# Zero-weight filler matmuls in TensorE's idle stretches of a two-block attention kernel

## The chip, the cores and the metric

The kernel runs on one core of one Trainium2 chip. The metric is device time in microseconds (us) from the first to the last instruction of the core, lower is better. A profiled span can differ from the median by some us, so each number below says which it is.

## The reference

Two blocks run twice each over a sequence of 2048 with 512 features. Block A is softmax attention with 32 query heads of 16 and one shared key/value head; block B is linear attention.

```python
def _A_ref(x, wq, wk, wv, wo):                 # H = 32, Dh = 16
    q = (x @ wq).reshape(B, S, H, Dh).transpose(0, 2, 1, 3)
    k, v = x @ wk, x @ wv
    p = softmax(einsum("bhqd,bkd->bhqk", q, k) * Dh ** -0.5)
    o = einsum("bhqk,bkd->bhqd", p, v)
    return o.transpose(0, 2, 1, 3).reshape(B, S, H * Dh) @ wo
def _B_ref(x, wqkv, wo):
    ...                                        # phi(q) (phi(k)^T v) / (phi(q) sum phi(k)), then @ wo
x = x + _A_ref(layernorm(x), ...)
x = x + _B_ref(layernorm(x), ...)
x = x + _A_ref(layernorm(x), ...)
x = x + _B_ref(layernorm(x), ...)
```

## The kernel before

A small scheduler in the kernel file plans the whole program before it is emitted. It keeps a model time, gives each operation a modelled duration, and starts on each free engine the ready operation of the best priority. The result is a fixed order for each engine, with semaphore waits between them. On the chip each engine runs its list in order. When TensorE (PE) is free in the model and events are left, it calls a hook:

```python
class Sched:
    def run(self):
        while True:
            ...                                # start what is ready
            if self.tfree[PE] <= self.now + 1e-9 and self.events:
                self.idle(self.now)
    ...
    def emit(self, name, eng):
        for o in self.order[name]:
            ...                                # waits
            ins = o.fn(eng)
            ...                                # semaphore increment
```

The attention work flows like this. PE makes up to three score tiles of 128x512 in PSUM banks 0-2 or 3-5. ScalarE (ACT) takes the exponential of all three at once into `PTA`. PE then multiplies them with V (the PV matmuls) into the accumulator bank 7. Some tiles go by bank 6 to VectorE (DVE), which makes the exponential into `PTD` with one operation for each tile (0.69 us in the page below) and six for a pair of tiles (0.42 to 1.21 us each). After 64 PV matmuls the bank is complete, and it is copied out to `Eo`. Until that copy is done no PV matmul of the next unit may start.

```python
# scores of m tiles, then one exponential
o  = add(PE, 0.05 + 0.14 * m, f, ..., prio=0.0, name="sA")
oe = add(AC, tac(m * 512), lambda e: e.activation(PTA[...], bank(3 * s, m * 512), ACTF.Exp, scale=SCALE), ...)
# PV, into 32 of the 128 partitions of bank 7
return e.matmul(ps[32 * c:32 * c + 32, 7 * 512:8 * 512], lhsT=Vaug[:, kt, :], rhs=src,
                start=opened[0], stop=opened[1], skip_group_check=True)
# the copy that frees bank 7
oe = add((DV, AC), ..., ev, deps=[last], acq=[he], uses=[h7], rel=[h7], prio=0.0, name="evA")

DUMMY = 0.0
def idle(now):
    if ctl.layer is None or ctl.ramp or ctl.tail or DUMMY <= 0:
        credit[0], credit[1] = 0.0, now
        return                                 # with DUMMY = 0 nothing is ever added
    ...
sc.idle = idle
```

The softmax here doesn't subtract the row's maximum and nothing guards it: scores larger than these inputs give would overflow.

## Time and profile before

| | before |
|---|---|
| time, three runs | 1869.71 us median (1867.76 to 1870.54) |
| profiled span, mean granted PE clock | 1878.3 us, 0.966 |
| start to first exponential | 15.4 us |
| first attention (start of the first to start of the last ACT exponential) | 888.7 us |
| layer tail and next start | 39.9 us |
| second attention | 888.3 us |
| last tail | 46.0 us |

These are lines of the profile page of the kernel before: busy time by engine, the granted clock in 40 slices, and two groups (line, engine, operation, names, shapes, count, then busy us, mean ns, and the idle time before them with what ended it).

```profile
PE 1656.9 (88%) x10339; PEld 487.6 (26%) x10408; DVE 1670.1 (89%) x2991; ACT 1738.2 (93%) x1525; POOL 33.7 (2%) x46
...
PEclk9999999996999989999899999999999998999998
...
L775 ACT ACTIVATE PTA<-ps_all 128x1536 bf16<-128x1536 f32 (+1 forms) x1265 | 1638.7, 1403 | 84.8 <-PE ps_all L635 79.2
L635 PE MATMUL ps_all<-QT,Kr 64*128 64x512 bf16 x4096 | 864.9, 392 | 135.5 <-ACT PTA L775 85.0
```

ACT is the fullest engine. PE's 88% should not be read as full: in this trace matmuls recorded as 392 ns long (the mean of L635) start some 215 to 227 ns apart at full clock, where they do not start together, so the records overlap. At half clock they start 390 to 426 ns apart. From these starts I estimate what PE's array does: I take a matmul as its columns at 2.4 for each ns (512 columns in the shortest steady spacing of 215 ns are 2.38) times the granted clock, and merge overlaps. By this estimate the array streams for about 1225 us of the 1878; with the median spacing of 222 ns it would be 1267. It counts the 256 float32 transposes of 128 columns short: in this trace they start 108 to 169 ns apart at full clock, not 53.

The clock records of the kernel before hold two levels only, 1.00 and 0.50. Its 17 stretches at 0.50 are 127 us together, and each, but for the last, which the trace's end cuts, is a whole number of 3.413 us long: one such length (3.41 us) to four (13.65 us), and one of ten (34.13 us). The stretches at full clock between them are whole numbers of it too. I call such a length a window, and the part of it that is covered by the estimate above its streaming share. The deepest dip of the clock line (the 6 in its tenth slice, about 423 to 470 us) is the stretch of ten windows; in it the array was covered to 0.72 to 0.89 of each window, and the clock stayed at 0.50 all the same. The next table looks there.

Here is the windows table of the kernel before (stretch and length, then busy us and count of PE, PEld, DVE, ACT, POOL, then granted clock, DMA share, GB/s). The first two stretches are slow ones, the third is calm.

```profile
430.00:440.00 10.00, 10.00 (x35) 1.57 (x32) 4.24 (x9) 5.80 (x4) 0.00 (x0) 0.50 0.00 0
440.00:450.00 10.00, 10.00 (x39) 1.84 (x38) 7.39 (x12) 7.82 (x6) 0.00 (x0) 0.50 0.00 0
580.00:590.00 10.00, 9.61 (x63) 2.80 (x61) 9.97 (x19) 10.00 (x9) 0.00 (x0) 1.00 0.00 0
```

At a clock of 0.50 PE looks fully busy, and ACT and DVE starve. The timeline of the kernel before shows why (start us, length us, engine, line, and count of the merged matmuls), first at half clock, then at full clock:

```profile
455.05 1.03 PE L635 MATMUL ps_all<-QT,Kr 64*128 64x512 bf16 x3
456.01 0.61 PE L671 MATMUL ps_all<-PTA,Vaug 128*32 128x512 bf16 x3
456.55 1.03 PE L635 MATMUL ps_all<-QT,Kr 64*128 64x512 bf16 x3
...
901.77 0.61 PE L635 MATMUL ps_all<-QT,Kr 64*128 64x512 bf16 x3 [0.42 <-ACT PTA L775]
902.31 0.40 PE L671 MATMUL ps_all<-PTA,Vaug 128*32 128x512 bf16 x3
```

At half clock one round of three scores and three PV takes 456.55 - 455.05 = 1.50 us, a little more than the 1.48 us exponential that it feeds (the mean of its form of 1536 columns), with nothing left for other work. At full clock PE has pauses, as the one of 0.42 us above.

And this is what came before a drop, in the timeline of the kernel before (the clock fell at 657.8):

```profile
655.38 0.60 PE L635 MATMUL ps_all<-QT,Kr 64*128 64x512 bf16 x4 [0.42 <-ACT PTA L775]
656.51 0.68 DVE L683 COPY Eo<-ps_all 128x512 f32<-128x512 f32 x1
657.25 0.09 PEld L671 LDWEIGHTS ps_all<-PTD,Vaug 128*32 128x32 bf16 x1 [1.75 <-DVE Eo L683]
657.25 0.39 PE L671 MATMUL ps_all<-PTD,Vaug 128*32 128x512 bf16 x1 [1.26 <-DVE Eo L683]
```

The accumulator is full, its copy to `Eo` starts late, and PE stands for 1.26 us. In the window before each of the twelve drops inside attention the longest pause of the array was 1.0 to 1.4 us for ten drops and 0.7 and 0.6 us for the other two, at a streaming share of 0.32 to 0.49.

### The profile page before, as it was taken

What the parts mean: (1) busy time and instruction counts of PE and PEld (TensorE: products, weight loads), DVE (VectorE), ACT (ScalarE), POOL (GpSimd) and SP (SyncE); (2) the same over time, 40 slices, a digit from 0 to 9 for tenths busy, and PEclk for the clock granted to TensorE, in tenths of its full rate; (3) what the DMA queues carried; (4) which work ended last, traced back from release to release, by engine and by line L of the source; (5) the groups of instructions that cost most, each with busy time, mean ns of one, the idle gap of its engine ahead of it and who ended that gap; (6) DMA issues with size and microseconds to landing.
All of it is one profiled execution on the core that took longest, in us unless ns stands there. A gap on an engine that the chain in (4) does not pass through costs nothing.

```text
span 1878.3 us, 25542 instructions
## 1 busy us (share of the span) xinstructions
PE 1656.9 (88%) x10339; PEld 487.6 (26%) x10408; DVE 1670.1 (89%) x2991; ACT 1738.2 (93%) x1525; POOL 33.7 (2%) x46
## 2 busy tenths in 40 slices
PE   7889899889998899899688899988989888998887
PEld 4222222221222223222342222222222222222223
DVE  7999989997889988998689999899998899989975
ACT  7999999997899989999689999999999999999995
POOL 0000000000000000000000000000000000000000
PEclk9999999996999989999899999999999998999998
DMA  3000000000000000000000000000000000000001
GB/s 113 1 1 1 1 1 1 1 1 1 1 1 1 1 1 1 1 1 1 0 1 1 1 1 1 1 1 1 1 1 1 1 1 1 1 1 1 1 1 45
DMA packets 7717, 9.00 MB, mean 5 GB/s; under 512 B 1456, under 2 KB 7088, under 8 KB 7600
## 3 DMA queue, kind: packets, MB, share of 16 engines
q1 hardware_dynamic: 7600, 7.37, 1.2%
q8 instruction: 81, 1.33, 0.3%
q14 instruction: 36, 0.29, 0.0%
HBM read 5.28 MB, written 2.10 MB: 4 GB/s over the span
## 4 chain that ended last, share of the span: by engine, by line
DVE 48%; PE 38%; ACT 10%; issue 2%; DMA 0%; POOL 0%; SPq 0%
PE ps_all L635 15%; PE ps_all L671 12%; DVE xT L829 11%; DVE PTD L851 9%; ACT PTA L775 9%; PE ps_all L496 7%; DVE xs L847 5%; DVE xs L850 5%; DVE xu L846 5%; DVE xu L849 3%; DVE xs L848 2%; PE ps_all L692 1%; DVE Eo L683 1%; DVE stats L461 1%; PE ps_all L1049 1%
## 5 line engine op out<-in xcount | busy, mean ns | idle before, releaser
L775 ACT ACTIVATE PTA<-ps_all 128x1536 bf16<-128x1536 f32 (+1 forms) x1265 | 1638.7, 1403 | 84.8 <-PE ps_all L635 79.2
L635 PE MATMUL ps_all<-QT,Kr 64*128 64x512 bf16 x4096 | 864.9, 392 | 135.5 <-ACT PTA L775 85.0
L671 PE MATMUL ps_all<-PTA,Vaug 128*32 128x512 bf16 x3567 | 559.5, 396 | 6.9 <-DVE Eo L683 5.0
L829 DVE TENSOR_SCALAR xT<-ps_all 128x512 int32<-128x512 f32 x529 | 362.3, 685 | 64.2 <-PE ps_all L635 62.0
L635 PEld LDWEIGHTS ps_all<-QT,Kr 64*128 64x128 bf16 x4096 | 179.5, 94 | 606.4 <-ACT PTA L775 283.9
L851 DVE SCALAR_TENSOR_TENSOR PTD<-xT,xs 128x1024 uint16<-128x1024 int32 x265 | 321.8, 1214 | 1.4
L671 PEld LDWEIGHTS ps_all<-PTA,Vaug 128*32 128x32 bf16 x3567 | 133.0, 93 | 485.7 <-issue 467.4
L846 DVE TENSOR_SCALAR xu<-xT 128x1024 f16<-128x1024 uint16 x265 | 181.8, 686 | 2.9
L850 DVE TENSOR_TENSOR xs<-xs,xu 128x1024 f16<-128x1024 f16 x265 | 180.8, 682 | 2.5
L847 DVE TENSOR_TENSOR xs<-xu 128x1024 f16<-128x1024 f16 x265 | 180.2, 680 | 1.4
L671 PE MATMUL ps_all<-PTD,Vaug 128*32 128x512 bf16 x529 | 148.5, 403 | 22.7 <-DVE Eo L683 16.9
L848 DVE TENSOR_SCALAR xs<-xs 128x1024 f16<-128x1024 f16 x265 | 110.3, 416 | 1.7
L849 DVE TENSOR_SCALAR xu<-xu 128x1024 f16<-128x1024 f16 x265 | 110.5, 417 | 0.0
L496 PE MATMUL ps_all<-wqkv_sb,xnT 128*128 128x512 bf16 x231 | 67.9, 398 | 6.1 <-issue 2.3
L469 POOL TENSOR_TENSOR rstd<-veps,mhalf 128x1 f32<-128x1 f32 x30 | 30.1, 1006 | 1764.6 <-DVE veps L467 1759.7
L671 PEld LDWEIGHTS ps_all<-PTD,Vaug 128*32 128x32 bf16 x529 | 32.1, 95 | 84.1 <-DVE Eo L683 28.9
L692 PE MATMUL ps_all<-identf,Eo 128*128 128x128 f32 x256 | 46.8, 311 | 6.2 <-DVE Eo L683 4.7
L928 ACT ACTIVATE e_buf<-ps_all 128x512 f32<-128x512 f32 x64 | 39.1, 610 | 12.9 <-PE ps_all L496 9.1
L683 DVE COPY Eo<-ps_all 128x512 f32<-128x512 f32 x62 | 42.4, 684 | 8.6 <-PE ps_all L671 8.5
L461 DVE BATCH_NORM_STATS2 stats<-x_sb 128x6 f32<-128x512 bf16 x64 | 42.9, 679 | 3.4 <-DMA x_sb<-in_A_x_dram 3.2
L929 DVE TENSOR_SCALAR e_buf<-e_buf 128x512 f32<-128x512 f32 x64 | 26.9, 420 | 20.7 <-ACT e_buf L928 20.6
L947 DVE CAST v_tok<-ps_all 128x512 bf16<-128x512 f32 x32 | 22.0, 688 | 25.0 <-PE ps_all L496 24.7
(85 smaller groups left out, 783.2 us busy)
## 6 DMA issues: line engine op xcount, KB each, us to landing
out_dram<-x_sb SPq DMA_DIRECT2D x16, 128.0 KB, 1.7
x_sb<-in_A_x_dram SPq DMA_DIRECT2D x3, 512.0 KB, 7.4
wqkv_sb<-in_B_wqkv_dram SPq DMA_DIRECT2D x1, 1536.0 KB, 11.8
x_sb<-in_A_x_dram SPq DMA_DIRECT2D x2, 256.0 KB, 3.1
wq_sb<-in_A_wq_dram SPq DMA_DIRECT2D x1, 512.0 KB, 5.1
wo_sb<-in_A_wo_dram SPq DMA_DIRECT2D x1, 512.0 KB, 9.2
wo_sb<-in_B_wo_dram SPq DMA_DIRECT2D x1, 512.0 KB, 10.9
wk_sb<-in_A_wk_dram SPq DMA_DIRECT2D x1, 16.0 KB, 2.5
```

The lines of the kernel that those rows point to most:

```text
L496: i = e.matmul(bank(h.idx, n), lhsT=l, rhs=r, start=(c + k == 0), stop=(c + k == len(mms) - 1))
L635: x = e.matmul(bank(b0 + k), lhsT=Kr[r, m, kt * P:(kt + 1) * P], rhs=QT[r, self.units[u][0] % 2, gs, q0:q0 + n], start=True, stop=True)
L671: return e.matmul(ps[32 * c:32 * c + 32, 7 * 512:8 * 512], lhsT=Vaug[:, kt, :], rhs=src, start=opened[0], stop=opened[1], skip_group_check ...
L692: i = e.transpose(bank(ht.idx, P, qs * P), Eo[:, he.idx, qs * P:(qs + 1) * P], identf[:])
L775: oe = add(AC, tac(m * 512), lambda e: e.activation(PTA[:, hp.idx, 0:m * 512], bank(3 * s, m * 512), ACTF.Exp, scale=SCALE), deps=[o] + pr ...
L829: o = add(DV, tdv(512), lambda e: e.tensor_scalar(out=xT[:, hx.idx, i * 512:(i + 1) * 512], in0=bank(6), scalar1=SCALE * LOG2E * 65536.0, ...
L846: o = add(DV, tdv(w, 0.52), lambda e: e.tensor_scalar(out=u_, in0=lo, scalar1=1.0 / 65536, scalar2=-0.5, op0=ALU.mult, op1=ALU.add), deps= ...
L847: o1 = add(DV, tdv(w, 0.52), lambda e: e.tensor_tensor(out=s_, in0=u_, in1=u_, op=ALU.mult), deps=[o] + c["prev"], name="xsq", **kw)
L848: o2 = add(DV, tdv(w, 0.26), lambda e: e.tensor_scalar(out=s_, in0=s_, scalar1=XK, scalar2=-XW, op0=ALU.mult, op1=ALU.add), deps=[o1], nam ...
L849: o3 = add(DV, tdv(w, 0.26), lambda e: e.tensor_scalar(out=u_, in0=u_, scalar1=1.0, scalar2=XL, op0=ALU.mult, op1=ALU.add), deps=[o1], nam ...
L850: o4 = add(DV, tdv(w, 0.52), lambda e: e.tensor_tensor(out=s_, in0=s_, in1=u_, op=ALU.mult), deps=[o2, o3], name="xc", **kw)
L851: o5 = add(DV, tdv(w), lambda e: e.scalar_tensor_tensor(out=PTD[:, hp.idx, 0:w].bitcast(U16), in0=xT[:, k, 0:w], scalar=2.0 ** -9, in1=s_, ...
```

## The change

The hook now adds filler matmuls: 512 columns of a finite constant tile, with 128x128 zero weights, into bank 7. The intent is to fill pauses like those before the drops. If the bank holds a running sum, the filler adds zero to it; if the bank is free, it starts a group there, and the first PV of the next unit overwrites it. A filler is planned where the model has PE idle and finds under 0.6 of the last 1.7 us streaming. It is not planned while the bank waits for its copy.

```diff
-    DUMMY = 0.0
+    FILL, FILLW, FILLN = 0.6, 1.7, 512
-    zer = sb("zer", [P, 240], BF16)
+    zer = sb("zer", [P, P], BF16)
+    def streaming(now):
+        tot = 0.0
+        for o in reversed(sc.order[PE]):
+            if o.t0 + 1.5 < now - FILLW:
+                break
+            st = {"pv": 0.071, "sA": 0.4, "dummy": 0.2}.get(o.name, 0.85 * o.dur[PE])
+            ...
+        return tot
     def idle(now):
-        if ctl.layer is None or ctl.ramp or ctl.tail or DUMMY <= 0:
-        ...
+        if not sc.order[PE] or streaming(now) > FILL * FILLW:
             return
         u = ctl.acc_owner
-        if credit[0] < 0.1 or u < 0 or not 0 < sum(ctl.count[u]) < 64:
+        owned = u >= 0 and 0 < sum(ctl.count[u]) < 64
+        if not owned and not banks.free[7]:
             return
+        if owned and now < sc.tfree[AC] < now + 0.1:
+            return
-        o = add(PE, 0.11, ... e.matmul(bank(7, 240, 272), lhsT=ident[:], rhs=zer[:], start=False, ...
+        o = add(PE, 0.03 + FILLN * 0.41e-3, lambda e: e.matmul(bank(7, FILLN), lhsT=zer[:],
+                rhs=maskx[:].bitcast(BF16)[:, 0:FILLN], start=not owned, stop=True, ...),
+                ..., prio=9.0, name="dummy")
```

Two things change: fillers run on PE, and their modelled 0.24 us shift the plan, so the order of the real work on PE, ACT and DVE is another one.

More of the change, by code (lines that the diff above doesn't have):

```diff
@@ L874, in bass_interleave_layers__grouped_kv_mqa__linear_attn_block__prompt_kernel @@
     sc.step = ctl.step
-    credit = [0.0, 0.0]
+    def streaming(now):
[4 more added lines that the diff above has]
+            st = {"pv": 0.071, "sA": 0.4, "dummy": 0.2}.get(o.name, 0.85 * o.dur[PE])
+            end = o.t0 + o.dur[PE]
+            if end > now - FILLW:
+                tot += st * min(1.0, (end - (now - FILLW)) / o.dur[PE])
+        return tot
     def idle(now):
-        if ctl.layer is None or ctl.ramp or ctl.tail or DUMMY <= 0:
-            credit[0], credit[1] = 0.0, now
+        if not sc.order[PE] or streaming(now) > FILL * FILLW:
             return
-        credit[0] = min(2.0, credit[0] + (now - credit[1]) * DUMMY)
-        credit[1] = now
         u = ctl.acc_owner
-        if credit[0] < 0.1 or u < 0 or not 0 < sum(ctl.count[u]) < 64:
+        owned = u >= 0 and 0 < sum(ctl.count[u]) < 64
+        if not owned and not banks.free[7]:
             return
-        credit[0] -= 0.1
-        o = add(PE, 0.11, lambda e: e.matmul(bank(7, 240, 272), lhsT=ident[:], rhs=zer[:], start=False, stop=True, skip_group_check=True),
-                reads=["ident", "zer"], prio=9.0, name="dummy")
+        if owned and now < sc.tfree[AC] < now + 0.1:
+            return
+        o = add(PE, 0.03 + FILLN * 0.41e-3, lambda e: e.matmul(bank(7, FILLN), lhsT=zer[:], rhs=maskx[:].bitcast(BF16)[:, 0:FILLN], start=not owned, stop=True, skip_group_check=True),
+                reads=["mask", "zer"], deps=[] if owned else list(banks.hist[7]), prio=9.0, name="dummy")
+        banks.hist[7].append(o)
         sc._try(PE)
```

## The prediction

> **What bounds the kernel now.** In the two attention stages (about 40–900 and 930–1826 us) ACT and DVE share the softmax exponentials and both are nearly full: the windows table gives ACT 97–98% and DVE 95–98% in calm stretches such as 560:650 and 1230:1300. TensorE (88% busy on the page) is not full: [...]I find its array idle for about 640 us of 1878. So TensorE matters only where it makes the others wait.
>
> It does so where its clock falls. The mean granted clock is 0.966; the clock records show about 17 stretches at exactly 0.50, together 127 us, nearly all 3.4 or 6.8 us long, one of 34 us (426:460). [...]the window before a drop was not empty: its streaming share was 0.32–0.49, where the mean of all windows is 0.65. At half clock three scores take 1.03 us on the timeline and not 0.60, three PV matmuls 0.61 and not 0.40, and one round of both takes 1.5 us, more than the 1.48 us exponential that it feeds.
>
> **What the drops cost.** In the twelve drops inside attention (plus 2.5 us of margin each) ACT idles 34 us and DVE 31 us where the calm rate would give 4–6; so about 27 us. The two layer tails (907:917, 1835:1856) run their serial chain at half clock: 4 transposes 0.61 us, projection matmuls 0.43 us each; about 3 us each, 6 us. Ceiling: some 33 us, 1.8%.
>
> **What the change adds.** Matmuls 128x512 of zero weights into bank 7, wherever the schedule's own model sees under 0.6 of the last 1.7 us streaming and TensorE idle. No work leaves. I estimate 500–1000 of them (attention alone models at about 0.5–0.55, the whole at 0.65), 0.215 us of array each, 110–215 us, against 640 us idle. [...] Estimated cost 3–12 us.
>
> **What it does not reach.** Most drops begin at a bank-7 turnover: TensorE waits 1.0–1.4 us for the DVE eviction (Eo, line 683; e.g. before 375, 426, 555, 658, 1313, 1562). Then bank 7 is neither owned nor free, so no filler may go there; only the rest of the 3.4 us window can be raised. I expect half-clock time to fall from 127 us to 20–60 us, not to nothing, and the long 34 us one to go. Gain 20–28 us, less cost 3–12.
>
> **Prediction.** 1852 us, 80% range 1830 to 1872. Faster by over 2%: 0.10; within 2%: 0.86; slower by over 2%: 0.04.
>
> **What would show it.** Right: mean clock 0.985 or more; half-clock time under 60 us; the exponential's idle before it (80 us on scores) falls by 15–25 us; ACT busy time unchanged. The filler group has 500–1000 instructions. Wrong: clock near 1 but time unchanged (then fillers delay scores: the exponential's waits for scores grow outside the former drops); or clock unchanged (then fillers sit at the wrong places[...]).
>
> **What would make it wrong.** The schedule model runs faster than the chip (its exponential is 1.37 us, the trace's 1.48), so fillers may land where the chip has no gap; the greedy schedule may shift as a whole by some us; more fillers than estimated; or a clock drop costing more than its own ACT idle.

Passages that no trace of this case shows are cut and marked, here and in the expectation of E4. No term of the sum is cut: the middles of 20 to 28 us gained and 3 to 12 us lost are 24 and 7.5, together some 16 us, from 1869 us to the forecast of 1852. The 640 us idle are read in the way told above (1878 less 1225 are 653).

## The result, and the profile after

The kernel after takes 1850.72 us median (1847.09 to 1853.99, four runs), the one before 1868.93 us beside it. The ratio is 0.9902 with a 95% interval of 0.9881 to 0.9922. By the 2% rule that is "same", and it is clear of noise.

| | before | after |
|---|---|---|
| profiled span, clock | 1878.3 us, 0.966 | 1845.4 us, 1.000 |
| start to first exponential | 15.4 | 14.5 |
| first attention | 888.7 | 874.0 |
| tail and next start | 39.9 | 35.7 |
| second attention | 888.3 | 879.6 |
| last tail | 46.0 | 41.6 |

The page of the kernel after, the same lines and the new group:

```profile
PE 1754.5 (95%) x11002; PEld 515.1 (28%) x11002; DVE 1658.7 (90%) x2966; ACT 1739.9 (94%) x1529; POOL 34.2 (2%) x46
...
PEclk9999999999999999999999999999999999999999
...
L775 ACT ACTIVATE PTA<-ps_all 128x1536 bf16<-128x1536 f32 (+1 forms) x1268 | 1640.6, 1398 | 59.4 <-PE ps_all L635 52.1
L635 PE MATMUL ps_all<-QT,Kr 64*128 64x512 bf16 x4096 | 835.1, 383 | 42.0 <-DVE xT L829 16.0
...
L897 PE MATMUL ps_all<-maskx,zer 128*128 128x512 bf16 x594 | 205.0, 387 | 0.0
```

ACT does the same work (1739.9 us, 1738.2 before) with less idle time before its exponentials (59.4 us, 84.8 before). The clock line has no dip. PE is busier by fillers, and its span is shorter all the same.

The windows table of the kernel after, at the stretches shown of before:

```profile
430.00:440.00 10.00, 10.00 (x60) 2.54 (x57) 9.41 (x16) 9.37 (x8) 0.00 (x0) 1.00 0.00 0
440.00:450.00 10.00, 9.11 (x55) 2.35 (x53) 9.97 (x17) 9.98 (x9) 0.00 (x0) 1.00 0.01 2
580.00:590.00 10.00, 9.88 (x56) 2.47 (x55) 9.90 (x17) 10.00 (x8) 0.00 (x0) 1.00 0.00 0
```

I also cut both traces into windows of 3.413 us (before, in step with the ends of its clock's stretches), and counted the windows at full clock, from the first exponential on, by their streaming share. Before, 23 had a share under 0.45 and 10 of those were followed by a drop; 45 had a share under 0.50, and 16 of those were followed by one. After, 4 and 8 are left, and none was followed by a drop. The lowest share rose from 0.19 to 0.41. (With the float32 transposes counted twice, the counts are 17 and 41 before, 1 and 5 after, with the same drops. With 222 ns for 512 columns they are 18 and 33 before, 10 and 14 of them followed by a drop, and 2 and 6 after, none of them. The reading does not hang on it, but the shares do by some hundredths.)

A copy of bank 7 still stops PE. In the timeline of the kernel after, around one of them:

```profile
372.03 0.60 PE L635 MATMUL ps_all<-QT,Kr 64*128 64x512 bf16 x3 [0.35 <-ACT PTA L775]
372.11 0.69 DVE L683 COPY Eo<-ps_all 128x512 f32<-128x512 f32 x1
372.85 0.42 PEld L692 LDWEIGHTS ps_all<-identf,Eo 128*128 128x128 f32 x4 [0.71 <-DVE Eo L683]
```

No filler stands there, as the rule demands: of the 594, none started during any of the 64 copies.

### The profile page after: what moved, and what is told of

Its sections match the earlier page's. It is cut to its first block, busy times and chain, and to the rows that moved or that the text cites. A ratio compares the mean times of both kernels' runs of the same rounds, so it can differ in the third digit from the quotient of the medians.

```text
span 1845.4 us, 26741 instructions
## 1 busy us (share of the span) xinstructions
PE 1754.5 (95%) x11002; PEld 515.1 (28%) x11002; DVE 1658.7 (90%) x2966; ACT 1739.9 (94%) x1529; POOL 34.2 (2%) x46
## 4 chain that ended last, share of the span: by engine, by line
PE 44%; DVE 43%; ACT 11%; issue 1%; POOL 1%; DMA 0%; SPq 0%
PE ps_all L635 17%; PE ps_all L671 13%; ACT PTA L775 10%; DVE xT L829 9%; DVE PTD L851 8%; PE ps_all L496 7%; DVE xs L850 5%; DVE xs L847 5%; DVE xu L846 4%; DVE xu L849 3%; DVE xs L848 2%; PE ps_all L897 2%; PE ps_all L692 1%; DVE Eo L683 1%; DVE stats L461 1%
## 5 line engine op out<-in xcount | busy, mean ns | idle before, releaser
L775 ACT ACTIVATE PTA<-ps_all 128x1536 bf16<-128x1536 f32 (+1 forms) x1268 | 1640.6, 1398 | 59.4 <-PE ps_all L635 52.1
L635 PE MATMUL ps_all<-QT,Kr 64*128 64x512 bf16 x4096 | 835.1, 383 | 42.0 <-DVE xT L829 16.0
L671 PE MATMUL ps_all<-PTA,Vaug 128*32 128x512 bf16 x3573 | 539.3, 389 | 3.4 <-DVE Eo L683 2.8
L851 DVE SCALAR_TENSOR_TENSOR PTD<-xT,xs 128x1024 uint16<-128x1024 int32 (+1 forms) x262 | 318.4, 1215 | 1.4
L897 PE MATMUL ps_all<-maskx,zer 128*128 128x512 bf16 x594 | 205.0, 387 | 0.0
L846 DVE TENSOR_SCALAR xu<-xT 128x1024 f16<-128x1024 uint16 (+1 forms) x262 | 180.2, 688 | 3.0
L850 DVE TENSOR_TENSOR xs<-xs,xu 128x1024 f16<-128x1024 f16 (+1 forms) x262 | 179.0, 684 | 3.0
L847 DVE TENSOR_TENSOR xs<-xu 128x1024 f16<-128x1024 f16 (+1 forms) x262 | 178.7, 682 | 2.0
L848 DVE TENSOR_SCALAR xs<-xs 128x1024 f16<-128x1024 f16 (+1 forms) x262 | 109.6, 418 | 2.1
L849 DVE TENSOR_SCALAR xu<-xu 128x1024 f16<-128x1024 f16 (+1 forms) x262 | 109.5, 418 | 0.0
L897 PEld LDWEIGHTS ps_all<-maskx,zer 128*128 128x128 bf16 x594 | 48.7, 96 | 105.0 <-issue 98.3
## 6 DMA issues: line engine op xcount, KB each, us to landing
wqkv_sb<-in_B_wqkv_dram SPq DMA_DIRECT2D x1, 1536.0 KB, 11.6
```

Of the source, the lines that this page charges most:

```text
L635: x = e.matmul(bank(b0 + k), lhsT=Kr[r, m, kt * P:(kt + 1) * P], rhs=QT[r, self.units[u][0] % 2, gs, q0:q0 + n], start=True, stop=True)
L775: oe = add(AC, tac(m * 512), lambda e: e.activation(PTA[:, hp.idx, 0:m * 512], bank(3 * s, m * 512), ACTF.Exp, scale=SCALE), deps=[o] + pr ...
L846: o = add(DV, tdv(w, 0.52), lambda e: e.tensor_scalar(out=u_, in0=lo, scalar1=1.0 / 65536, scalar2=-0.5, op0=ALU.mult, op1=ALU.add), deps= ...
L847: o1 = add(DV, tdv(w, 0.52), lambda e: e.tensor_tensor(out=s_, in0=u_, in1=u_, op=ALU.mult), deps=[o] + c["prev"], name="xsq", **kw)
L848: o2 = add(DV, tdv(w, 0.26), lambda e: e.tensor_scalar(out=s_, in0=s_, scalar1=XK, scalar2=-XW, op0=ALU.mult, op1=ALU.add), deps=[o1], nam ...
L849: o3 = add(DV, tdv(w, 0.26), lambda e: e.tensor_scalar(out=u_, in0=u_, scalar1=1.0, scalar2=XL, op0=ALU.mult, op1=ALU.add), deps=[o1], nam ...
```

## The experiments

There were twelve runs in three sets of four. Each set has its own chip and its own runs of the kernel before, whose means were 1873.3, 1873.0 and 1869.6 us. Every run had a right result. "Half-clock us" is 2 x (1 - granted clock) x span: the clock records of the kernel before show only 1.00 and 0.50, and the same two levels are taken for every run.

My theory: fillers hold the clock, and the clock gives the time. Rivals: the new order gives the time and the clock comes with it; fillers are free; any PE instruction does.

### E1: the kernel before again

No edit.

> The kernel before, once more, to read the granted clock of each of its runs. The one profiled run stood at 0.966 and was 10 us longer than the timed ones. Theory (the gain is the clock): the timed runs stand near 0.975, and the time falls with the clock from run to run, by 3 to 5 us for each 0.01. Ratio 1.000.

Measured: six runs, 1868.95 to 1877.81 us, ratio 0.9993 (0.9967 to 1.0019), clock 0.968 to 0.974. With the eleven paired runs of before, these 17 runs of one program give a straight line:

time = 1835.3 us + 0.354 x (half-clock us), correlation 0.94.

The half-clock time lies between 93 and 128 us, with means of 104 (this kernel's runs) and 107 (the paired ones). Why runs of the same program differ in it was not shown. The forecast missed the slope: it said 3 to 5 us for each 0.01 of clock, and 0.354 makes 13 us. The line is read over a narrow range, and 1835 us at full clock is an extrapolation with a standard error of 3.6 us; the next runs test it. (The paired runs of before of the other two sets, on other chips, lie on the same line: all 39 runs give 1836.7 + 0.342 x, with standard errors of 2.0 and 0.020.) Below, "at full clock" means the measured mean less 0.354 x its half-clock us.

### E2: the new order, without fillers

```diff
-            ins = o.fn(eng)
+            ins = o.fn(eng) if o.name != "dummy" else None
```

> The order of the kernel after on every engine, with its 594 fillers planned but not emitted. Theory (fillers hold the clock): the clock falls back to 0.96-0.98 and the time to 1862-1880 us, ratio 0.997 or more. Rival (the plan, which reserves idle TensorE time, gives a better order, and the clock comes with it): the time stays at 1846-1856 us, ratio 0.99.

Measured: 1860.76 us median (1854.42 to 1869.75), ratio 0.9941 (0.9911 to 0.9972), clock 0.974 to 0.984, half-clock 76 us. The median falls between the two forecasts, and the ratio is lower than the 0.997 that the theory gave: neither forecast was right. At full clock it is 1835.5 us, as before. So the order does a part, some 10 us (106 - 76 half-clock us, times 0.354), and it does it by the clock: it has fewer low windows (counted in the profiled runs, 21 under 0.45, against 24 in E1; 7 under 0.40, against 11). The rest of the kernel after's gain, from a ratio of 0.994 to 0.990, would be the fillers' in this order; the two ran in different sets and their intervals touch, so E3 is the cleaner test.

### E3: the old order, with fillers

Fillers are planned with no duration, and no two within 0.24 us. Compared operation by operation, the order of the real work is that of the kernel before on every engine, with 582 fillers put between.

```diff
-        if not sc.order[PE] or streaming(now) > FILL * FILLW:
+        if not sc.order[PE] or streaming(now) > FILL * FILLW or now < ctl.filled + 0.24:
...
-        o = add(PE, 0.03 + FILLN * 0.41e-3, lambda e: ...
+        ctl.filled = now; o = add(PE, 1e-6, lambda e: ...
```

> The order of the kernel before on every engine, unchanged, with 582 fillers put between by the same rule (planned with no duration). Theory (fillers hold the clock): clock 0.99 or more, 1844-1856 us, ratio about 0.99. Rival (order): about 1868 us, ratio 1.00, or worse by the fillers' own cost of 3-12 us.

Measured: 1855.99 us median (1853.15 to 1859.12), ratio 0.9903 (0.9877 to 0.9929), clock 0.995 to 0.999, half-clock 11 us. Fillers with zero weights alone hold the clock (0.997 on average, where the paired runs of before have 0.971) and give the whole gain in an unchanged order. The rival of order falls as the main cause. At full clock the kernel would be at 1852.1 us, 17 us over the 1835 of the same order without fillers: the first sign that fillers are not free.

### E4: fillers of 16 columns

```diff
-    e.matmul(bank(7, FILLN), lhsT=zer[:], rhs=maskx[:].bitcast(BF16)[:, 0:FILLN], ...
+    e.matmul(bank(7, 16), lhsT=zer[:], rhs=maskx[:].bitcast(BF16)[:, 0:16], ...
```

> The kernel after with each filler cut from 512 columns to 16, at the same 594 places and in the same order. Theory[...]: the fillers' array time falls from some 127 us to 4 us, the clock falls to 0.96-0.98, 1862-1880 us. Rival (any TensorE instruction that breaks up a pause counts): clock 0.99 or more, and 1840-1852 us as the fillers cost less.

Measured: 1861.42 us median (1859.75 to 1864.74), ratio 0.9938 (0.9914 to 0.9962), clock 0.977 to 0.982, half-clock 73 us. The time is just under the theory's range and far from the rival's: just E2 again, though 594 weight loads and matmuls stand at the same places. In this order the clock stood at 0.998 on average with 594 fillers of 512 columns, at 0.980 with 594 of 16 columns, and at 0.980 with none: it went with the columns streamed, not with the number of instructions. At full clock it is 1835.8 us, so 594 short instructions cost nothing that shows. That speaks for the long ones costing by their length too.

### E5: each filler twice

```diff
-            ins = o.fn(eng)
+            ins = [o.fn(eng) for _ in range(1 + (o.name == "dummy"))][-1]
```

> The kernel after, each filler issued twice, 1188 of them, same order. From the runs so far: the kernel before lies on time = 1835 + 0.35 x (half-clock us), and the plan without fillers on 1835 + 0.35 x too, while the kernel after ran 1847 at full clock. So theory: fillers cost some 12 us of their own, and the doubled ones cost 12 to 20 us more at clock 1.00: 1859-1870 us. Rival (fillers lie in true gaps and cost nothing; the straight line is misleading, as the drops fall where stalls are anyway): 1845-1852 us.

Measured: 1914.65 us median (1914.55 to 1919.50), ratio 1.0229 (1.0200 to 1.0258), clock 0.997 to 1.000. The direction is the theory's, the size is not: I expected 12 to 20 us more and got 64. These are waits at the scores (who waited for whom, us in total, times, longest us), first of the kernel after, then of the doubled one:

```profile
ACT PTA L775 <- PE ps_all L635: 52.1, 127, 1.5
DVE xT L829 <- PE ps_all L635: 45.7, 88, 1.5
...
PE ps_all L635 <- ACT PTA L775: 13.3, 49, 0.7
```

```profile
ACT PTA L775 <- PE ps_all L635: 93.4, 245, 1.9
DVE xT L829 <- PE ps_all L635: 83.4, 178, 1.5
...
PE ps_all L635 <- ACT PTA L775: 5.9, 21, 0.7
```

The clock was full in both (1.000), so this is the fillers' own cost: PE reaches ready score matmuls late, and ACT and DVE wait about 40 us more each. ACT's busy time grew too, from 1739.9 to 1758.5 us, with the same 1529 instructions. They took no longer (added up singly, 1901.0 us and then 1878.4), so they overlap each other less; the two make about 60 of the 67 us by which the profiled span grew. The last line of each is the opposite wait, PE for ACT before scores. It is PE's slack. In this one order it was, without fillers (E2):

```profile
PE ps_all L635 <- ACT PTA L775: 102.1, 287, 0.9
```

and then 13.3 us in the kernel after and 5.9 in the doubled one. These sums are rough: 71 of 10408 matmul records are missing from E2's trace and 175 of 11596 from the doubled one's.

### E6: threshold 0.5

```diff
-    FILL, FILLW, FILLN = 0.6, 1.7, 512
+    FILL, FILLW, FILLN = 0.5, 1.7, 512
```

> The threshold of the filler rule at 0.5 and not 0.6: 321 fillers planned. Theory (a gain by the clock less a cost by the filler, about 0.02 us each): cost falls to some 6 us, and if the clock stays at 0.99 or more the time is 1842-1850 us, a little better than the kernel after. If the clock falls to 0.985: 1852-1856. Rival (fillers cost nothing): same or slower than the kernel after.

Measured: 1837.76 us median (1835.53 to 1841.68), ratio 0.9816 (0.9788 to 0.9844), clock 0.994 to 0.998, half-clock 15 us. That is better than forecast, and the best of all runs. The kernel after had a ratio of 0.9902 (0.9881 to 0.9922); the two intervals do not meet, though the two did not run side by side. The profiled run's waits for PE's scores are little shorter than those of the kernel after, with 273 fillers fewer:

```profile
ACT PTA L775 <- PE ps_all L635: 50.2, 121, 1.8
DVE xT L829 <- PE ps_all L635: 41.2, 75, 1.3
```

They are 2 and 4.5 us shorter, where the profiled span is 11.6 us shorter; ACT's busy time is 6.1 us less (1733.8 against 1739.9). So these waits do not show where most of the gain comes from. The waits of PE itself are not compared here, as a part of this trace's matmul records is missing: it has 234 matmul records of the fillers and 321 weight loads, and 321 were planned. I took the counts of fillers from the plan and the loads.

### E7: threshold 0.4

The edit is as in E6, with 0.4.

> The threshold at 0.4: 139 fillers planned. The windows before a drop had a streaming share of 0.32 to 0.49, so some drops should come back: clock 0.980 to 0.992, time 1844-1858 us.

Measured: 1841.18 us median (1838.33 to 1846.04), ratio 0.9832 (0.9803 to 0.9862), clock 0.988 to 0.994, half-clock 33 us. That is better than forecast (1844 to 1858 us). With 139 fillers the clock is mostly held. At full clock it is 1830.3 us, 5 us under the line of before, so a cost of the fillers can't be read here: this plan's order may be better by itself.

### E8: no fillers in starts and tails

```diff
-        if not sc.order[PE] or streaming(now) > FILL * FILLW:
+        if ctl.layer is None or ctl.ramp or ctl.tail or not sc.order[PE] or streaming(now) > FILL * FILLW:
```

> The kernel after, with no fillers planned in the start-up stretches and the layer tails (522 of 594 left). Theory: the drops in the two tails come back (27 us of half clock, clock 0.985) and cost by the prediction 6 us, by the measured stages 4 + 4 us: 1855-1860 us. Rival (the tails gain nothing, since they wait for ACT and DVE): 1848-1852 us.

Measured: 1861.09 us median (1860.56 to 1862.08), ratio 0.9934 (0.9909 to 0.9959), clock 0.989 to 0.992, half-clock 37 us. That is about 10 us over the kernel after, where 4 + 4 were expected, and 1 us over the forecast. The windows table of this run at its two tails, and then that of the kernel after at its own:

```profile
891.00:908.00 17.00, 9.82 (x49) 4.90 (x50) 6.50 (x18) 3.08 (x8) 0.00 (x0) 0.60 0.00 0
1816.00:1833.00 17.00, 9.91 (x47) 4.71 (x48) 7.53 (x22) 3.92 (x8) 0.00 (x0) 0.60 0.00 0
```

```profile
885.00:905.00 20.00, 16.07 (x99) 6.26 (x97) 7.75 (x22) 8.81 (x14) 0.00 (x0) 1.00 0.00 1
1800.00:1820.00 20.00, 16.20 (x99) 6.35 (x98) 7.48 (x21) 8.82 (x14) 0.00 (x0) 1.00 0.01 1
```

The clock falls there again, to 0.60 on average against 1.00. The tail between the attentions takes 41.1 us (35.7 in the kernel after) and the last one 45.6 us (41.6): 5.4 + 4.0 us of serial chain. E8 is a new plan, so its order is not quite that of the kernel after; E2, which has that order and no fillers, loses 3.2 + 3.7 us in the same stretches (38.9 and 45.3 us). At full clock E8 is at 1848.2 us, like the kernel after (1848.0): the half-clock time accounts for all of the difference.

### E9: the order of after, every second filler

```diff
-            ins = o.fn(eng)
+            ins = o.fn(eng) if o.name != "dummy" or o.idx % 2 else None
```

> The order of the kernel after on all engines, but only the 295 fillers at odd places of TensorE's order are emitted. So far the same order ran 1862 with none (clock 0.980), 1850 with all (0.998) and 1915 with all twice (1.000); with the clock's part taken off (0.35 us for each us of half clock) 1835, 1847 and 1915. Theory (cost grows with the fillers, faster than their number): 1837-1842 us at full clock, 1838-1848 as measured, clock 0.990 or more. Rival (the win of the 0.5 threshold came from its other order, not from fewer fillers): 1846-1852 us.

Measured: 1855.41 us median (1852.45 to 1857.17), ratio 0.9920 (0.9900 to 0.9940), clock 0.989 to 0.991, half-clock 36 us. As a time this is a miss, 7 us over the top of the forecast, for the clock fell more than a range up to 1848 allows. At full clock it is 1841.9 us, as the theory said. So in one and the same order:

| fillers emitted | half-clock us | mean us | at full clock | cost of fillers |
|---|---|---|---|---|
| 0 (E2) | 76 | 1862.3 | 1835.5 | - |
| 594 of 16 columns (E4) | 73 | 1861.7 | 1835.8 | 0 |
| 295 (E9) | 36 | 1854.8 | 1841.9 | 6 |
| 594 (after) | 7 | 1850.6 | 1848.0 | 12 |
| 1188 (E5) | 5 | 1916.4 | 1914.7 | 79 |

The last column is the one before less 1835.5. Taking away blindly half of the fillers gives back in clock (29 us x 0.354 = 10 us) more than it saves (6 us). So E6's gain over the kernel after does not follow from a smaller number alone: which ones stay, or the order of E6's own plan, must matter. The runs of this table come from four sets; the line takes out the clock's part of what differs between them. The step from 594 to 1188 is between two kernels at nearly full clock, while the 6 and the 12 rest on the line.

### E10 to E12: other fillings

E10 has threshold 0.45 in attention and 0.6 elsewhere; E11 has threshold 0.5 with fillers of 256 columns; E12 has threshold 0.45 everywhere.

```diff
-        ... streaming(now) > FILL * FILLW:
+        ... streaming(now) > (0.6 if ctl.layer is None or ctl.ramp or ctl.tail else 0.45) * FILLW:     # E10
-    FILL, FILLW, FILLN = 0.6, 1.7, 512
+    FILL, FILLW, FILLN = 0.5, 1.7, 256                                                             # E11, "dummy": 0.1
+    FILL, FILLW, FILLN = 0.45, 1.7, 512                                                            # E12
```

> Threshold 0.45 in attention, 0.6 in the start-up stretches and the layer tails: 229 fillers planned. Theory: fillers in the tails cost nothing and those in attention do, so clock 0.993 or more and 1832-1840 us, as good as threshold 0.5 everywhere or a little better.

> Threshold 0.5 with fillers of 256 columns, 518 of them, in place of 321 of 512. Theory (a filler costs by standing in front of a ready matmul, so by its length): same clock (0.996), 2 to 5 us less: 1832-1838 us. Rival (cost by the instruction and its weight load): 2 to 6 us more, 1840-1845 us.

> Threshold 0.45 everywhere: 191 fillers planned. Between the 0.4 run (1841, clock 0.991) and the 0.5 run (1838, clock 0.996): clock 0.993-0.996, 1833-1842 us.

| run | fillers | median us | ratio | half-clock us | at full clock |
|---|---|---|---|---|---|
| E10 | 229 | 1841.79 (1837.47 to 1844.58) | 0.9848 (0.9823 to 0.9874) | 26 | 1832.3 |
| E11 | 518 short | 1845.95 (1844.82 to 1848.30) | 0.9874 (0.9851 to 0.9898) | 21 | 1838.7 |
| E12 | 191 | 1850.24 (1847.83 to 1856.45) | 0.9903 (0.9879 to 0.9926) | 40 | 1836.7 |

All three missed their range upwards, E12 by most. E12 should lie between E6 and E7 and is slower than both. Each threshold makes another plan, and these orders differ by some us at full clock (1830.3 to 1836.7 among E6, E7, E10 and E12, in no order of the filler count) and in half-clock time (15 to 40 us). So the threshold's optimum is not a smooth one, and I can't tell the part of fewer fillers from the part of a lucky order in E6. E11 leaves open whether shorter fillers are better, for the same reason.

## Why the prediction was right

**The time.** 1852 us forecast, 1850.72 measured, inside the range, and "within 2%" was right with 0.86. But the gain by the clock was put too small and the cost of the fillers came out at the top of its range; the two errors partly offset each other, so a miss of only 1.3 us is in part luck.

**What bounds the kernel.** Right. ACT's busy time is the same before and after, and ACT and DVE gained where PE's clock had fallen (in 430 to 440 us ACT is busy for 9.37 us, 5.80 before, and DVE for 9.41 us, 4.24 before). E1 shows it without any change: the same program's time follows its half-clock time.

**What the drops cost.** Too small. I read 33 us from idle time in the profiled run. That run had 127 half-clock us, and the slope of 0.354 makes that 45 us there; for an average run with 106 it makes 38 us. The tails were the clearest part: I said 3 us each, and the stages show 4.2 (39.9 to 35.7) and 4.4 (46.0 to 41.6), E8 about 10 us for starts and tails together.

**What half-clock time stays.** This step failed. The prediction said that "only the rest of the 3.4 us window can be raised. I expect half-clock time to fall from 127 us to 20–60 us". As to the copies it was right: no filler started in any of the 64. Yet half-clock time fell to 0 in the profiled run and 7 us on average of the four. Raising the rest was enough: the lowest windows went up to 0.41 to 0.50, and none of the 8 under 0.50 brought a drop, where 16 of 45 had done so before. The new order took away a part too (E2: 76 us, where before has 106).

**What fillers cost.** The count was right (594, forecast 500 to 1000). The forecast of their cost was an estimate without a measurement behind it. The cost of 12 us in this order is at the top of the forecast of 3 to 12, and in the old order it is over it: 17 us (E3).

**The sum as measured.** Clock: (106 - 7) x 0.354 = 35 us gained (106 is the mean of the 17 runs of before), of which the order alone has about 10 us (E2). Fillers: 12 us lost. Together 23 us, against 1872.9 - 1850.6 = 22 us between the means of before (17 runs) and after (4 runs, another set); side by side it was 18.5 us, as those runs of before were faster. That the sum closes is no test of it: the cost is what the line leaves. The order of the kernel after by itself, at equal clock, gives nothing that shows: 1835.3 and 1835.5 us. Other orders may give some us, as E6, E7 and E10 lie 2 to 5 us under the line although they have fillers. The forecast had 20 to 28 gained and 3 to 12 lost.

**The signs.** Clock above 0.985: 0.996 to 1.000. ACT's idle time on scores falls by 15 to 25 us: it fell by 27 (79.2 to 52.1). The 34 us stretch is gone; it is a matter of chance in the run too, for E1's longest is 17 us.

**What stays open.** The line's intercept is an extrapolation, supported by E2 and E4 (1835.5 and 1835.8 us with less half-clock time) but by no filler-free run at full clock. Why the second 594 fillers cost five times the first is argued, not shown part by part: in the kernel after PE has 13 us of waits for ACT before scores left, so more fillers find little slack. What part of E6's gain is fewer fillers and what part another order stays open too.

## What to carry to other kernels

When the clock records of an engine that isn't the bottleneck show drops, as here 17 stretches at 0.50 for 127 us, look at them before calling its pauses free: run the same program several times and regress time on half-clock time (here 0.354 us for each), which gives an estimate of the worth of a full clock without any edit. If fillers are to hold the clock, as 582 did here in an unchanged order (0.971 to 0.997), count them as work of their own (6 us for 295, 12 for 594 and 79 for 1188, read with the line), place as few as keep the low windows up, and check by emitting none and twice as many in the same order. When a plan is made by a model, separate what is added from the reordering that the addition causes.
